# Attention over chosen chunks and a gated feed-forward: twenty-two loads issued by GpSimd in joined packets, and a new order table

## Chip, cores and metric

The kernel runs on one core of a Trainium2 chip. The metric is device time in microseconds of one execution; a profiled execution shows, beside its own time, the span from the first to the last instruction of the program. The engines are TensorE (PE; its weight loads are listed as PEld), VectorE (DVE), ScalarE (ACT), GpSimd (POOL) and SyncE (SP), which only issues transfers. Each engine works off its own queue in order. Transfers run on 16 DMA engines that all queues share.

## What is computed

Inputs are q, k, v of shape 4 x 8 x 768 x 64 (batch, heads, sequence, head size), and the weights of a feed-forward with 512 inputs and 1536 hidden values, all in float32.

```python
k_min, k_max = k_chunks.min(axis=3), k_chunks.max(axis=3)      # 24 chunks of 32 keys
ub = sum(maximum(q * k_min, q * k_max), axis=-1)               # bound of each query on each chunk
ub = where(causal, ub, -1e9); top_chunks = argsort(ub)[..., -6:]
scores = where(sel & (pos[:, None] >= pos[None, :]), scale * q @ k.T, -1e9)
x = softmax(scores) @ v                                        # as 3072 tokens x 512
out = (sigmoid(x @ w_gate) * (x @ w_val)) @ w_out
```

So each query attends, causally, to the six chunks with the highest bounds, and the result goes through the gated feed-forward.

## The kernel before

The 24 blocks of 128 queries (4 batches of 6) are put into eight units u0 to u7 of three blocks (u2 has two of its own and one more). The first block of each batch needs no choice of chunks; the functions `load_first` and `first` handle it. The first blocks of batches 0 to 2 are u0, that of batch 3 is joined to u2. For a unit the stages are:

- load queries and keys; turn them so that the head size lies on the partitions. u1 and u2 (batch 0) are loaded in wide rows (`load_wide`, tiles k0_u1 to q3_u2), copied (kn, qn) and turned on TensorE (kT, qT). Batches 1 to 3 are loaded in blocks of 32 x 32 (`load_blocks`, k00_1 to q11_3, runs of 128 B) and turned on VectorE.
- smallest and largest key of each chunk (kx, kcr), the bounds (ub), the six largest (mx), and from these a bias that is written beside the queries as extra rows (hqm) and meets a pattern beside the keys (hkp), so that the score product itself puts chunks out that were not chosen.
- scores (sc), exponent on ScalarE (exp), causal mask on GpSimd (cm), sums with the values (pv; the values are loaded by `load_v` as v_b_i and cast on GpSimd as v16), division (rz, x), turn (xps, xT).
- feed-forward: gate product g, value product v_u, tanh on ScalarE, product hg on VectorE, output product o0 to o2 in three pieces, eviction osb, store out. Weights come as wg0 to wg2, wv0 to wv2, wo0 to wo2, 512 KB each as landed, cast to float16 on their way by transfers that GpSimd issues. u4 with u5, and u6 with u7, share their gate and value products in a scheme with seven products in place of eight.

For a first block of batch b: kf0, kf1, qf0, qf1 (halves of the heads) and vf are its loads, kfT and qfT the turns, scm and scf mask and scores, expf, pvf, rzf, xf, xpsf, xTf the rest as above; xTf copies the result into u0's input.

Every step is entered with `plan.add(name, {engine: cost...}, emit, ...)`. Nothing is planned at run time: the text `ORDER` lists all 1893 entries by name, with the engine behind `@` where it is not the first one given in `add`, and behind `:` the slots of the buffers that the entry is the first to use. `plan.order()` emits them in that order, and each engine's queue is the sequence of its own entries. The costs in `add`, and the due times `prio`, were used to draw the table and do not act otherwise. Buffers matter for loads: there are two large landing buffers (`big`: u1, u2, and then the key and query blocks of a batch) and six for values and first blocks (`v`); a load whose buffer still has readers waits, and the loads behind it on that queue wait with it.

In the table before, SP issues 107 transfers: all key, query and value loads and all stores but the last. GpSimd issues only the nine weights. The first gate product, g_u0_0, has 54 TensorE entries ahead of it, among them twelve score groups of u1; wg0 and wv0 stand at places 21 and 23 of GpSimd's queue.

## Time and profile before

| | |
|---|---|
| median of 3 runs | 287.46 us (287.25 to 287.63) |
| profiled execution | 287.56 us, span 285.8 us |
| HBM read, written | 30.67 MB, 6.29 MB |
| SP's queue: packets, MB, share of 16 engines | 118448, 27.47, 45.3% |
| GpSimd's queue: packets, MB, share of 16 engines | 4752, 4.72, 10.2% |
| granted TensorE clock | 0.998 |

How to read the views: busy time is the union of an engine's instructions. Idle time is put down to what released the engine. The 40 slices of a row show the busy share of each slice in tenths, a slice being 7.1 us. A row of the view by stretch gives start and end, length, then busy time and count for PE, PEld, DVE, ACT and POOL, the granted clock, the DMA share and GB/s. A row of a tile or line gives the shortest, median and longest duration in ns and the first and last start in us, and "to landing" the time from an issue to the end of its transfer.

### The profile page before, as it was taken

To read this page: it belongs to the slowest core of one execution; us is meant where nothing else is said; L and a number is where in the kernel's file an instruction comes from. 1 tells how busy PE (TensorE), PEld (TensorE's weight loads), DVE (VectorE), ACT (ScalarE), POOL (GpSimd) and SP (SyncE) were. 2 spreads that over 40 slices of the span, in tenths; PEclk is the share of its full clock that TensorE was granted. 3 is DMA by queue.
4 is the path that set the end of the run, shared out by engine and by line. 5 is a ranking of instruction groups with operands and counts; after the bars stand their busy time and mean duration, and the time that the engine had idled before them with its cause. 6 is when DMAs were issued, how large, how long until landed. Compare 5 with 4: busy or idle time off the path is not lost.

```text
span 285.8 us, 7062 instructions
## 1 busy us (share of the span) xinstructions
PE 268.1 (94%) x2626; PEld 170.8 (60%) x2626; DVE 230.8 (81%) x626; ACT 213.2 (75%) x452; POOL 120.7 (42%) x199
## 2 busy tenths in 40 slices
PE   1677899999999899999999999999999999999995
PEld 0554566656666557777657776665667555555542
DVE  3588967659996998898978988898998778799842
ACT  4979887667858798989998978689899324766311
POOL 6479688214672688875674732350212000000000
PEclk9999999999999999999999999999999999999999
DMA  6999999999999999998031000100000020100005
GB/s 167 278 225 204 208 209 209 212 174 197 181 214 148 212 214 214 217 181 149 30 85 74 4 2 0 39 37 2 38 3 2 0 110 2 73 37 3 0 17 204
DMA packets 123377, 32.69 MB, mean 114 GB/s; under 512 B 111440, under 2 KB 120400, under 8 KB 123344
## 3 DMA queue, kind: packets, MB, share of 16 engines
q1 hardware_dynamic: 118448, 27.47, 45.3%
q0 software_dynamic: 4752, 4.72, 10.2%
q8 instruction: 20, 0.33, 0.5%
q14 instruction: 13, 0.11, 0.1%
q10 hardware_dynamic: 144, 0.07, 0.1%
HBM read 30.67 MB, written 6.29 MB: 129 GB/s over the span
## 4 chain that ended last, share of the span: by engine, by line
PE 74%; DMA 5%; SPq 4%; DVE 3%; ACT 3%; issue 1%; POOL 0%; DVEq 0%
PE o_u L962 19%; PE sc_u L848 10%; PE v_u L931 8%; PE g_u L931 8%; PE pv_u L881 6%; SPq L537 3%; PE sug_u6u L1041 3%; PE suv_u6u L1041 3%; PE sug_u4u L1041 3%; PE suv_u4u L1041 3%; DMA k<-in_k_dram 2%; DMA q<-in_q_dram 2%; PE ube_u L787 2%; PE xps_u L908 1%; PE srv_u6u L1041 1%; PE srg_u6u L1041 1%
## 5 line engine op out<-in xcount | busy, mean ns | idle before, releaser
L859 ACT ACTIVATE att_u<-sc_u 128x512 f16<-128x512 f32 (+3 forms) x184 | 91.4, 556 | 16.2 <-PE sc_u L848 15.0
L962 PE MATMUL o_u<-wo,hg_u 128*128 128x512 f16 x216 | 52.8, 379 | 0.0
L865 POOL TENSOR_SCALAR_AFFINE_SELECT att_u<-att_u 128x384 f16<-128x384 f16 (+1 forms) x56 | 29.1, 529 | 48.7 <-ACT att_u L859 45.8
L931 PE MATMUL v_u<-xT_u,wv 128*128 128x384 f16 x192 | 39.1, 326 | 0.0
L931 PE MATMUL g_u<-xT_u,wg 128*128 128x384 f16 x192 | 39.0, 326 | 0.0
L962 PEld LDWEIGHTS <-hg_u 128*128 128x128 f16 x216 | 20.4, 98 | 20.1 <-issue 0.6
L939 ACT ACTIVATE gate_u<-g_u 128x384 f16<-128x384 f32 x48 | 23.7, 498 | 8.7 <-PE g_u L931 8.5
L943 DVE SCALAR_TENSOR_TENSOR hg_u<-gate_u,v_u 128x384 f16<-128x384 f16 x48 | 25.3, 539 | 5.6 <-PE v_u L931 2.3
L848 PE MATMUL sc_u<-hqe,hke 128*128 128x128 f16 (+2 forms) x220 | 28.7, 243 | 1.2 <-DVE kx_u L561 0.9
L848 PE MATMUL sc_u<-hqo,hko 128*128 128x128 f16 (+2 forms) x220 | 27.6, 243 | 0.5 <-DVE hg_u L943 0.5
L881 PE MATMUL pv_u<-v,att_u 128*128 128x65 f16 x640 | 27.3, 193 | 0.7 <-POOL att_u L865 0.6
L881 PEld LDWEIGHTS <-att_u 128*128 128x128 f16 x640 | 24.7, 98 | 4.9 <-POOL att_u L865 1.1
L931 PEld LDWEIGHTS <-wv 128*128 128x128 f16 x192 | 17.8, 98 | 10.5 <-issue 0.5
L931 PEld LDWEIGHTS <-wg 128*128 128x128 f16 x192 | 18.0, 98 | 10.0
L848 PEld LDWEIGHTS <-hke 128*128 128x128 f16 x220 | 16.7, 98 | 6.8 <-issue 1.6
L848 PEld LDWEIGHTS <-hko 128*128 128x128 f16 x220 | 16.8, 98 | 6.3 <-ACT att_u L859 0.6
L971 ACT ACTIVATE osb_u<-o_u 128x512 f32<-128x512 f32 x17 | 10.1, 606 | 9.3 <-PE o_u L962 9.3
L962 PE MATMUL o_u<-wo,hgp_u 128*128 128x512 f16 (+1 forms) x72 | 17.0, 370 | 0.0
L553 POOL CAST v<-v 128x512 f16<-128x512 f32 x23 | 13.8, 611 | 4.1 <-DMA v<-in_v_dram 3.8
L900 DVE TENSOR_TENSOR x_u<-pv_u,rz_u 128x384 f16<-128x384 f32 (+1 forms) x28 | 14.6, 528 | 0.7 <-PE xps_u L908 0.3
L342 ACT COPY xT_u<-xps_u 128x384 f16<-128x384 f16 (+1 forms) x22 | 10.1, 474 | 5.2 <-PE xps_u L908 5.1
L346 POOL CAST k<-k 128x768 f16<-128x768 f32 x9 | 7.5, 833 | 13.9 <-DMA k<-in_k_dram 13.8
(215 smaller groups left out, 597.3 us busy)
## 6 DMA issues: line engine op xcount, KB each, us to landing
v<-in_v_dram SPq DMA_DIRECT2D x23, 256.0 KB, 4.5
out_dram<-osb_u SPq DMA_DIRECT2D x23, 256.0 KB, 2.1
k<-in_k_dram SPq DMA_DIRECT2D x12, 384.0 KB, 6.8
q<-in_q_dram SPq DMA_DIRECT2D x12, 384.0 KB, 5.4
wg<-in_moe_w_gate_dram POOLq DMA_DIRECT2D x3, 512.0 KB, 8.9
wv<-in_moe_w_val_dram POOLq DMA_DIRECT2D x3, 512.0 KB, 10.0
wo<-in_moe_w_out_dram POOLq DMA_DIRECT2D x3, 512.0 KB, 9.1
kf<-in_k_dram SPq DMA_DIRECT2D x8, 128.0 KB, 3.4
```

The source lines that it names most:

```text
L342: nc.scalar.copy(o, i)
L553: plan.add(f"v16_{b}_{ib}", {POOL: pool(H * D)}, lambda e: nc.gpsimd.tensor_copy(v16[b % 2][:, ib, :, 0:D], at(t)), reads=[t], writes=[("v ...
L848: nc.tensor.matmul(at(t)[:, o:o + 128 * m], hk[b % 2][e_][:, p, 128 * jb:128 * jb + 128], hq[u.side][e_][:, p, 128 * x:128 * (x + m)], sta ...
L859: plan.add(f"exp_{u.name}_{h}_{y}", {ACT: act(n)}, lambda e, t=t, att=att, b0=b0, n=n: nc.scalar.activation(at(att)[:, b0:b0 + n], at(t), ...
L865: nc.gpsimd.affine_select(out=dv, in_=dv, compare_op=ALU.is_ge, fill=0.0, base=0, pattern=[[0, u.m], [1, 128]], channel_multiplier=-1)
L881: nc.tensor.matmul(at(pv)[:, last, x, :], at(att)[:, c:c + 128], v16[b % 2][:, jb, h, :], start=(jb == 0), stop=(jb == ib))
L900: plan.add(f"x_{u.name}_{p}", {DVE: dve(u.t)}, lambda e: nc.vector.tensor_tensor(at(x_).rearrange("p a (e d) -> p e a d", e=2), at(pv)[:, ...
L931: nc.tensor.matmul(at(t), w16[:, c, 128 * fb:128 * fb + 128], at(u.xt)[:, c, :], start=(c == 0), stop=(c == 3))
L939: plan.add(f"tanh_{u.name}_{fb}", {ACT: act(T)}, lambda e, g=g, gate=gate: nc.scalar.activation(at(gate), at(g), AF.Tanh, scale=0.5), read ...
L943: plan.add(f"hg_{u.name}_{fb}", {DVE: dve(T)}, lambda e, w_=w_, gate=gate, hg=hg: nc.vector.scalar_tensor_tensor(at(hg), at(gate), 1.0, at ...
L962: nc.tensor.matmul(at(o), hgs[c][1][1]()[:, 128 * tb:128 * tb + 128], wo16[:, fc, lo:hi], start=(c == 0), stop=(c == NFB - 1))
L1041: nc.tensor.matmul(at(t), left[i](c), right[i](c), start=first and c == 0, stop=c == 1, skip_group_check=not first)
```

## The change

Three helpers that issue loads now take an engine: a load by GpSimd is issued with `single_packet=True`, so that the pieces which one DMA engine has to move are joined in one packet. Which loads go there is written in the table. The table itself is drawn anew: 185 of the 1893 entries change their engine (22 of them loads), and nearly all their places.

```diff
+    def read(e, o, i):
+        if e == SP:
+            nc.sync.dma_start(o, i)
+        else:
+            nc.gpsimd.dma_start(o, i, single_packet=True)
...
-                plan.add(f"{n}f_{b}", {SP: (550, 550)}, lambda e, t=t[n], src=src: nc.sync.dma_start(
+                plan.add(f"{n}f_{b}", {SP: (550, 550), POOL: (930, 930)}, lambda e, t=t[n], src=src: read(e, 
...
-                    plan.add(f"{n}f{e_}_{b}", {SP: (550, 550)}, lambda e, t=t[n], src=src, e_=e_: nc.sync.dma_start(
+                    plan.add(f"{n}f{e_}_{b}", {SP: (550, 550), POOL: (750, 750)}, lambda e, t=t[n], src=src, e_=e_: read(e, 
...
-                plan.add(f"{'kq'[j]}{p}_{u.name}", {SP: (450, 450)}, lambda e, j=j, p=p, src=src: nc.sync.dma_start(
+                plan.add(f"{'kq'[j]}{p}_{u.name}", {SP: (450, 450), POOL: (800, 800)}, lambda e, j=j, p=p, src=src: read(e, 
...
-        plan.add(f"v_{b}_{ib}", {SP: (450, 450)}, lambda e: nc.sync.dma_start(
+        plan.add(f"v_{b}_{ib}", {SP: (450, 450), POOL: (930, 930)}, lambda e: read(e, 
```

The start of the table, before and after (the first load of each, and the place of the first weights and of the first products of the feed-forward):

```diff
-tri0 ap1 ident epat0:0 ident16 tri k2_u1:0 kn_u1_2:0 kT_u1_2:0 kt_u1_2:0 q1_u2:1 vf1_1:1 epat kcr0 kx0_u1_2
...
-hq1_u1_2@POOL wv0 apt0_u1:0 rzf_1_1:1 xf_0_0:0 hk1_u1_0@ACT kn_u2_2:6 qf16_3:0 hq0_u1_1 expf_0_1:1 kT_u2_2:6 kx0_u2_2
...
-wv1 cm_u1_1 v16_0_1 kx0_u2_0 v16_0_3 exp_u1_2_1 g_u0_0:4,0,0 exp_u1_0_2 tanh_u0_0 kfT_3:7 v_u0_0:3 mx1_u1 kx0_u2_3
+hq0 epat0:0 k1_u1:0 ident kn_u1_1:0 kT_u1_1:0 v10 k0_u2:1 kf1_2:0 kf0_2 q1_u1 k0_u1@POOL kn_u1_0:1 q2_u1@POOL kf1_0:1
+epat kn_u2_0@POOL:2 hkp001 qf1_0:2 q1_u2 hkp101@ACT kT_u2_0:1 kt_u2_0@DVE:0 kx1_u2_0:0 qn_u1_1@POOL:3 qT_u1_1:2 hk0_u2_0
...
+hkf1@ACT kT_u1_3:0 kx1_u1_3 expf_0_0 qT_u2_1:3 qf1_3:5 qf1_1 wg0 hk0_u1_0@ACT pvf_0_0:4 expf_0_1:2 hq1 qfT_1:2 qT_u2_0:7
...
+vc_1 qn_u2_2:1 qfT_2:2 xpsf_0_0:7,0 qf16_2:5 wv0 kx0_u1_3 kt_u1_3@DVE:2 xTf_0_0 kcr_u1@POOL qm_u1_1@ACT qm_u1_0@ACT
...
+hqm0_u1_0 kf0_3@POOL:0 g_u0_0:3,0,0 v_u0_0:1 g_u0_1:4,1,1 kt_u2_1@DVE:2 kx1_u2_1 ubn1_u1 v_u0_1:2 hkf0@ACT hkp110@ACT
...
+qm_u2_1@ACT qm_u2_2@ACT k11_1:0 v_0_2:5 v_u0_3:6 tanh_u0_3 exp_u1_2_2 v_0_3:1 kf1_3 exp_u1_2_0 hkp010 hg_u0_2 hg_u0_3
```

In queue order, GpSimd's loads are k0_u1, q2_u1, k2_u2, qf0_0, q0_u2, qf0_1, q2_u2, qf0_2 (all ahead of wg0), q3_u2 (ahead of wv0), kf0_3, v_0_1, vf_3, v_0_4, v_1_2, v_1_0 and seven more values of batches 1 to 3. wv1 and wg1 follow wv0 with three entries of other work among them. SP keeps 85 transfers; behind its first 24 loads come k11_1, v_0_2, v_0_3 and kf1_3. g_u0_0 has 42 TensorE entries ahead of it, none of them scores of u1; v_u0_0 comes right behind it.

More of the change, by code (lines that the diff above doesn't have):

```diff
@@ new lines @@
+vc_1 qn_u2_2:1 qfT_2:2 xpsf_0_0:7,0 qf16_2:5 wv0 kx0_u1_3 kt_u1_3@DVE:2 xTf_0_0 kcr_u1@POOL qm_u1_1@ACT qm_u1_0@ACT
+scm_2:4,1 pvf_0_1:0 pvf_1_0:6 pvf_1_1:7 scf_2:2 qT_u2_2:2 kxf1:1 expf_2_0 k1_u2 rzf_0_1:1 xf_0_1:1 xpsf_0_1:5 pvf_2_0:0
+rzf_1_1:0 xf_1_1:2 xTf_0_1 wv1 rzf_1_0:1 hk0_u1_2@POOL qf16_3:4 rzf_2_0:0 xf_2_0:0 xpsf_1_1:4 kT_u2_3:7 expf_2_1:3
+qf_u2_2 hq0_u1_1@POOL pvf_2_1:3 xTf_1_1 wg1 xf_1_0:1 rzf_2_1:0 hkp100 kcr_f@POOL xpsf_2_0:5 kn_u2_1@DVE:3 xf_2_1:2
+xTf_2_0 ub_u1:1,0 qm_u2_0@POOL:0 xpsf_1_0:2 ubn0_u1:0 xpsf_2_1:4 xTf_2_1 hk0_u1_3@POOL hk1_u1_3@POOL hq1_u2_2 hkp011@ACT
@@ new lines @@
+exp_u1_1_0 sc_u1_0_0:5,0 exp_u1_0_0 qm_u2_3@ACT sc_u1_0_2:4 sc_u1_3_2:3 g_u0_4:2,1,4 sc_u1_3_1:7 v_u0_4:1 exp_u1_3_1
+exp_u1_0_2 sc_u1_1_2:0 sc_u1_0_1:5 g_u0_5:6,0,5 v_u0_5:7 exp_u1_3_2 exp_u1_1_2 tanh_u0_5 sc_u1_2_1:4 sc_u1_1_1:3 hg_u0_5
+wv2 ub_u2:0,6 tanh_u0_4 exp_u1_1_1 g_u0_6:2,2,6 v_u0_6:7 g_u0_7:3,3,7 ap1_u1 apt1_u1 hg_u0_4 exp_u1_0_1 ubn1_u2:0
+ubn0_u2 hq1_u1_1@DVE exp_u1_2_1 hqm1_u1_0@ACT cm_u1_0 tanh_u0_6 hqm1_u1_2@ACT cm_u1_1 k10_1 mx1_u2:0 hq0_u2_0@POOL
+cm_u1_3 v16_0_1 v16_0_3 v16_0_2 pv_u1_0:5 tanh_u0_7 pv_u1_1 sc_u1_4_1:4,0 sc_u1_7_2:1,3 sc_u1_4_0:0 exp_u1_7_2
@@ L270 @@
+P3v_u6u7_5 C1v_u6u7_5 o1_u6_0 o1_u6_2 P4v_u6u7_5 o1_u7_1 hg_u6u7_1_11 hg_u6u7_1_5 o2_u7_1 hg_u6u7_0_11 o0_u7_0:0,1
+o1_u7_0 o2_u7_0 hg_u6u7_0_5 o2_u6_2 o0_u7_2:5,2 osb_u7_0@DVE out_u7_0 osb_u6_2 out_u6_2 o2_u6_0 osb_u6_0@DVE osb_u7_1
+out_u7_1 out_u6_0 o2_u6_1 osb_u6_1 out_u6_1 o1_u7_2 o2_u7_2 osb_u7_2@DVE out_u7_2 o0b_u7_2:6 o1b_u7_2 o2b_u7_2 osbb_u7_2
+outb_u7_2@ACT
 """
```

328 lines of the change are left out of this document (156 added, 172 removed).

## The prediction

> **What bounds the kernel now.** I read the page first (busy times, the 40 slices), then busy time by stretch, then the timeline at the places where TensorE waits, and last the landings of single loads.
>
> ```profile
> span 285.8 us, 7062 instructions
> PE 268.1 (94%) x2626; PEld 170.8 (60%) x2626; DVE 230.8 (81%) x626; ACT 213.2 (75%) x452; POOL 120.7 (42%) x199
> PE   1677899999999899999999999999999999999995
> DMA  6999999999999999998031000100000020100005
> ```
>
> ```profile
> 0.00:33.00 33.00, 20.06 (x191) 13.80 (x192) 22.30 (x69) 26.64 (x51) 23.96 (x48) 1.00 0.97 218
> 33.00:50.00 17.00, 16.96 (x210) 11.29 (x209) 12.68 (x56) 14.44 (x34) 12.38 (x23) 1.00 1.29 207
> 50.00:130.00 80.00, 78.80 (x843) 51.60 (x841) 67.98 (x202) 63.82 (x136) 47.66 (x76) 1.00 1.08 197
> 130.00:180.00 50.00, 50.00 (x625) 33.93 (x624) 43.88 (x123) 44.06 (x89) 26.36 (x40) 1.00 0.18 44
> 180.00:280.00 100.00, 99.94 (x745) 58.75 (x744) 82.11 (x179) 63.96 (x143) 10.37 (x16) 1.00 0.07 27
> 280.00:285.80 5.80, 2.36 (x21) 1.44 (x19) 1.90 (x3) 0.28 (x1) 0.00 (x0) 0.92 0.60 226
> ```
>
> The columns of the second view are the stretch, its length, then busy us of TensorE matmuls, weight loads, VectorE, ScalarE and GpSimd, the granted clock, the DMA share and GB/s. TensorE is the bound: of 17.7 us in which it does nothing (285.8 - 268.1), 12.94 lie in the first 33 us, 1.20 between 50 and 130 us and 3.44 behind 280 us. The arithmetic is the same in the changed kernel, so its time is this TensorE work plus whatever idle time the new order leaves. The end (last output products, eviction, store) keeps its form in the new table; its 3.44 us I leave as they are. What can move is the head, and the 1.20 us.
>
> The head is bound by loads and by the engines that turn them, in this way:
>
> ```profile
> 0.00:5.00 5.00, 0.88 (x3) 0.50 (x3) 1.54 (x5) 1.86 (x3) 3.62 (x11) 1.00 0.48 128
> 5.00:10.00 5.00, 1.37 (x7) 1.38 (x8) 1.74 (x4) 4.44 (x6) 1.33 (x2) 1.00 1.03 285
> 10.00:15.00 5.00, 3.99 (x24) 2.95 (x22) 3.75 (x9) 4.58 (x8) 3.31 (x5) 1.00 1.08 256
> ```
>
> ```profile
> 5.45 0.56 DVE L561 TENSOR_REDUCE kcr<-kT_u 128x12 f32<-128x384 f32 x1 [2.90 <-ACT kt_u L342]
> ...
> 32.51 0.27 DVE L344 COPY xT_u<-xpsf 128x256 f16<-128x256 f16 x1
> ```
>
> ```profile
> 33.00 0.81 PE L931 MATMUL g_u<-xT_u,wg 128*128 128x384 f16 x4
> 33.65 0.60 PE L589 MATMUL kfT<-ident,kf 128*128 128x128 f32 x4
> 34.26 0.82 PE L931 MATMUL v_u<-xT_u,wv 128*128 128x384 f16 x4
> 34.92 0.81 PE L931 MATMUL g_u<-xT_u,wg 128*128 128x384 f16 x4
> ```
>
> From 5 us on the DMA engines are full; only the first 5 us have room (share 0.48), because one queue, SP's, issues everything. The first gate product g_u0_0 starts at 33.00 us, just behind the last piece of its input that VectorE copies (32.51 + 0.27); the first value product v_u0_0 at 34.26 us, just behind its weights:
>
> ```profile
> L492 POOL DMA_DIRECT2D wg<-in_moe_w_gate_dram x1: 995/995/995, 21.8 to 21.8; - x1
> ...
> DMA to landing us min/median/max: 9.1/9.1/9.1
> ```
>
> ```profile
> L493 POOL DMA_DIRECT2D wv<-in_moe_w_val_dram x1: 751/751/751, 23.3 to 23.3; - x1
> ...
> DMA to landing us min/median/max: 10.9/10.9/10.9
> ```
>
> ```profile
> L492 POOL DMA_DIRECT2D wg<-in_moe_w_gate_dram x1: 740/740/740, 31.4 to 31.4; - x1
> ...
> DMA to landing us min/median/max: 7.3/7.3/7.3
> ```
>
> ```profile
> L493 POOL DMA_DIRECT2D wv<-in_moe_w_val_dram x1: 747/747/747, 32.1 to 32.1; - x1
> ...
> DMA to landing us min/median/max: 10.0/10.0/10.0
> ```
>
> wg0 lands at 21.8 + 9.1 = 30.9, wv0 at 23.3 + 10.9 = 34.2; wg1 at 38.7, wv1 at 42.1. So a weight of 512 KB lands 7.3 to 9.1 us after its issue with nothing ahead of it on Pool's queue, and 3.3 to 3.4 us after the one ahead of it otherwise. From 33 us on TensorE is full (16.96 of 17.00).
>
> **The change, part by part. (a) Loads to Pool.** SP loses 22 of its 107 entries, Pool gains 22. Price on SP, and the nearest on Pool:
>
> ```profile
> L527 SPq DMA_DIRECT2D kq_u<-in_k_dram x8: 435/469/505, 0.8 to 20.9; - x8
> L547 SPq DMA_DIRECT2D v<-in_v_dram x23: 375/803/4636, 22.0 to 142.4; - x23
> L492 POOL DMA_DIRECT2D wg<-in_moe_w_gate_dram x3: 740/788/995, 21.8 to 41.1; - x3
> ```
>
> No load of this kind was ever issued by Pool here, nor one in joined packets. I take 0.8 us each, by the weights' median, with 0.74 and 0.995 as ends: 17.6 us of Pool's time (16.3 to 21.9). In the table Pool hands over 25 other entries (ScalarE +7, VectorE +18), at some 0.5 us each about 12 us, so Pool goes from 120.7 to about 126 us, VectorE from 231 to about 238 of 286: each has room on average, and this part costs nothing while TensorE has other work ready. What waits behind a Pool issue are Pool's casts and causal masks; in the head, eight loads stand before wg0.
>
> On how the two queues share the engines: the Trainium skill, "DMA: Bandwidth & Descriptors", section "Issuing engines are not separate DMA queues", says that transfers issued by any engine run on the same 16 DMA engines and that a second issuer only saves sequencer time. By that rule the move buys no bandwidth beyond the half empty first 5 us, and the case of no change below is the one it speaks for; the share of 1.03 to 1.08 in the rows from 5 to 15 us agrees.
>
> **(b) The head in the new order.** Pool's queue up to wg0: 14 entries that are not loads, by their rows about 9.5 us (the two pattern fills 2.0, one mask copy 1.46, one clamp 1.0, the rest 0.3 to 0.6), eight loads at 0.8 make 6.4, the start at 0.8 us, and about 1 us of waiting for a query load and for a turned query: wg0 is issued at 17.6 instead of 21.8. Then a cast, two small fills, one query copy and one load, some 2.2 us, and wv0 goes at about 20.7. wg0 lands at 24.9 to 26.7, wv0 3.3 later, at 28.2 to 30.0. The other condition is the last copied piece of the input: VectorE has 58 entries to do up to there, against 60 before. Without a single wait behind the first turned tile this is 5.45 + (22.30 - 1.54), or 26.2 us; with every wait of before 32.8. I take the middle, 29.5, because loads land earlier but the chain load, turn, copy, score, exp, sum, divide, turn, copy is as long as it was. g_u0_0 then starts at 29.5 and v_u0_0 at 30.15 with its weights there.
>
> That is not all gain: the new order does less TensorE work before v_u0_0. Twelve score groups of u1 and one turn of keys, which stood ahead, now come behind.
>
> ```profile
> 0.00:33.00 33.00, 3.29 (x24) 1.85 (x24) 1.00 0.97 218
> ```
>
> This is busy time of the scores' line alone in the head: 3.29 us for these 24 matmuls. Streaming alone they need less, 12 groups of 384 columns on average at 0.16 us (a product of four such matmuls takes 0.65, 34.92 less 34.26), or 1.95. With 0.60 for the turn of keys the start that would change nothing is 34.26 - 0.60 - (1.95 to 3.29), or 30.4 to 31.7, middle 31.0. So the head gives **0.85 us** (ends: v_u0_0 at 33.45, if VectorE waits as it did, is a loss of 3.0 against 30.4; at 28.2 it is a gain of 3.5 against 31.7).
>
> **(c) Weights in a row.** wv1 and wg1 are issued at about 21.8 and 23.6, not 32.1 and 31.4, so four weights run in a row. At 3.3 apart they land at about 32.4 and 35.7. g_u0_4 needs wg1; it stands behind v_u0_0, six more products (4.55 with it) and seven score groups (1.9 by 3.29 / 12 each): 30.15 + 6.45 = 36.6. It is just in time: cost 0, or 2.5 us at a spacing of 5 (rival C).
>
> **(d) Keys and values of the later units.** k11_1, the first block load of keys (128 B runs), may start as soon as u1's landing buffer is free and the 24 loads ahead of it on SP are issued (at 0.47 to 0.80 us each 11 to 19 us), say at 18 us; v_0_2, v_0_3 and kf1_3 queue behind it on SP; before, these values went ahead of it.
>
> ```profile
> L537 SPq DMA_DIRECT2D k<-in_k_dram x1: 1431/1431/1431, 33.4 to 33.4; - x1
> ...
> DMA to landing us min/median/max: 14.6/14.6/14.6
> ```
>
> ```profile
> L537 SPq DMA_DIRECT2D k<-in_k_dram x4: 1431/6047/12317, 33.4 to 55.2; - x4
> ...
> DMA to landing us min/median/max: 7.5/16.4/24.2
> ```
>
> By 14.6 us beside weights it lands at 32.6, the two values by 35 (256 KB at 212 GB/s is 1.2 us each), and pv_u1_0, which needs them cast, is due near 43: cost 0; at 24.2 it is not (rival D).
>
> **(e) The middle.** Eleven of the values no longer stand in SP's queue among key and query blocks, so a block that TensorE waited for in 80 to 100 us can come sooner. Of the 1.20 us I count 0.35 as gained (ends: all 1.20, or a loss of as much again, since the whole table is drawn anew).
>
> **Sum.** -0.85 - 0.35 = -1.2 us. The profiled execution took 287.56 us (span 285.8 and 1.76 around it), 0.10 above the median of 287.46. So 287.56 - 1.2 - 0.10 gives **286.3 us**.
>
> **Rivals. A, larger gain:** VectorE runs with few waits (28.0) and v_u0_0 starts at 28.6: 2.4 in the head, 1.2 in the middle, 283.9. For it: loads come from two queues in the first 5 us. Against it: DMA is full from 5 us on.
>
> **B, no change:** the head is bound by bytes, whoever issues them; earlier weights only take from the loads that feed VectorE, which waits as long as before, less what the first 5 us give. 287.4.
>
> **C, slower, weights pile up:** wg1, fourth in a row beside loads and key blocks, holds g_u0_4, with all of TensorE behind it. It decides from a spacing of 3.75 us (36.6 less 29.1 for wv0, halved for two weights); at 5 us wg1 lands at 39.1, 2.5 late: 287.5 - 1.2 + 2.5 = 288.8. For it: the pair wg1, wv1 took 10.7 us before. Against it: 3.3 and 3.4 between neighbours.
>
> **D, slower, values behind k11_1:** at 24.2 us it lands at 42.2, the values at 44.6, two casts of 0.61 in Pool's order end at 45.8, some 2.8 late for pv_u1_0 at 43, and Pool's masks with them: 289.1. It decides from a landing behind some 39 us.
>
> ```profile
> L553 POOL CAST v<-v 128x512 f16<-128x512 f32 x23 | 13.8, 611 | 4.1 <-DMA v<-in_v_dram 3.8
> ```
>
> **E, slower, Pool pays more or the middle loses:** an issue costs over 0.995 because Pool is held up, or the redrawn middle adds idle time: 1 to 3 us; with 2 of it, and the head's 0.85 kept, 288.6. The Trainium skill, "SBUF — State Buffer", section "SBUF: two separate sides", warns that descriptors made by GpSimd starve while VectorE runs a two-port copy; it quotes 620 ns becoming 3100, which as an estimate from that page would put some 2.5 us on an unlucky issue. The spread here, 740 to 995 ns beside a busy VectorE, is a tenth of that.
>
> **Chances.** The forecast as told (285.4 to 286.8) 0.26, A 0.18, B 0.13, C 0.15, D 0.15, E 0.13. A measurement of this kernel can tell some 0.2%, 0.57 us, from no change. So faster 0.44, same 0.13, slower 0.43. Range 283.7 to 290.5: it takes in all but the far ends of A, C, D and E.
>
> **What would show it.** v_u0_0 at 30.2 or before with more than 20 us of TensorE work done by 33 us bears out (b); wv0 landing by 30 and wg1 by 36 bear out (c); no wait of TensorE at the first sums of u1 near 43 bears out (d); Pool's loads at 0.74 to 1.0 us bear out (a). The forecast is wrong if TensorE idles over 0.5 us between 33 and 50 us, if Pool's issues take over 1.2 us, or if the idle time of 50 to 180 us grows over 2 us.

## The result, and the profile after

| | before | after |
|---|---|---|
| median, 20 executions each | 286.82 us (285.26 to 288.20) | 288.59 us (286.49 to 290.06) |
| profiled execution, span | 287.56 us, 285.8 us | 288.12 us, 286.4 us |

The ratio of after to before is 1.006 [1.0041, 1.0079]: the change makes the kernel slower, by 1.2 to 2.3 us. The 20 executions of before put its median at 286.82 us, 0.64 below the 287.46 of the three from which the prediction added up. The two profiles differ by less, 0.56 us: the profiled execution of before lies 0.7 us above its median, that of after 0.5 us below. A second profile of before, taken with the experiments, has a span of 284.4 us, and both are used below.

Busy times of after, and the row of TensorE over 40 slices:

```profile
span 286.4 us, 7079 instructions
PE 268.5 (94%) x2626; PEld 170.9 (60%) x2626; DVE 236.7 (83%) x644; ACT 218.3 (76%) x459; POOL 122.9 (43%) x196
PE   2778899989998999999999999999999999999995
DMA  7999999999999879279140200103000020002005
```

The head of the row is fuller than before (2778 against 1677), and a few slices behind it are not. The view by stretch of after, with the columns of before, says how much:

```profile
0.00:33.00 33.00, 22.05 (x192) 14.45 (x193) 24.74 (x77) 26.42 (x49) 26.60 (x48) 1.00 1.07 233
33.00:50.00 17.00, 16.37 (x195) 11.16 (x193) 12.46 (x53) 15.46 (x38) 12.38 (x23) 1.00 1.27 225
50.00:130.00 80.00, 76.80 (x857) 50.56 (x852) 70.50 (x197) 66.96 (x143) 50.16 (x76) 1.00 0.95 176
130.00:180.00 50.00, 50.00 (x621) 33.91 (x620) 46.09 (x141) 40.31 (x80) 23.18 (x34) 1.00 0.24 55
280.00:286.40 6.40, 3.23 (x26) 1.93 (x24) 1.25 (x2) 0.94 (x3) 0.00 (x0) 1.00 0.59 222
```

TensorE is idle 10.95 us of the first 33 against 12.94 before, 0.63 against 0.04 from 33 to 50, and 3.20 against 1.20 from 50 to 130 us. The head gives and the middle takes. The middle again, 40 to 130 us, first of before and then of after:

```profile
40.00:130.00 90.00, 88.78 (x982) 58.20 (x980) 74.73 (x231) 71.81 (x155) 55.67 (x91) 1.00 1.11 198
```

```profile
40.00:130.00 90.00, 86.80 (x997) 57.85 (x997) 79.53 (x232) 76.47 (x165) 56.63 (x88) 1.00 0.99 181
```

In these 90 us VectorE has 4.8 us more to do and ScalarE 4.7 (79.53 - 74.73, 76.47 - 71.81). TensorE waits for them, and for late loads that reach it through them. The waits of TensorE, from the timeline of after (start, busy us, instruction, and in brackets the idle time ahead of it and who ended it):

```profile
29.93 0.50 PE L937 MATMUL v_u<-xT_u,wv 128*128 128x384 f16 x2 [0.90 <-DMA wv<-in_moe_w_val_dram]
36.50 0.50 PE L937 MATMUL g_u<-xT_u,wg 128*128 128x384 f16 x2 [0.63 <-ACT att_u L865]
63.35 0.37 PE L887 MATMUL pv_u<-v,att_u 128*128 128x65 f16 x7 [0.83 <-POOL v L559]
81.31 0.28 PE L854 MATMUL sc_u<-hqe,hke 128*128 128x256 f16 x1 [0.36 <-DVE hqe L344]
92.19 0.32 PE L854 MATMUL sc_u<-hqo,hko 128*128 128x384 f16 x1 [0.89 <-POOL hqo L346]
95.04 0.34 PE L914 MATMUL xps_u<-ident,x_u 128*128 128x128 f16 x3 [0.46 <-DVE x_u L906]
123.48 0.32 PE L937 MATMUL v_u<-xT_u,wv 128*128 128x384 f16 x1 [0.66 <-DVE hg_u L949]
```

The last five, 63 to 123 us, make 3.20 us. Before had only two waits of TensorE behind 33 us (line waited for, total us, times, longest us):

```profile
PE pv_u L881 <- POOL att_u L865: 0.6, 1, 0.6
PE sc_u L848 <- DVE hg_u L943: 0.5, 1, 0.5
```

Three of the five can be followed back. The wait at 63 us goes back to the value v_0_5, for which GpSimd's casts waited. Its row and landing (the longest of the loads of values in this window) are

```profile
L507 SPq DMA_DIRECT2D v<-in_v_dram x1: 1702/1702/1702, 55.3 to 55.3; - x1
DMA to landing us min/median/max: 4.8/5.8/6.8
```

SP issued it at 55.3, behind three blocks of keys, and it landed at 62.1. The wait at 92 us begins at VectorE:

```profile
87.97 0.98 DVE L567 TRANSPOSE_TENSOR_REDUCE kcr<-k 128x24 f32<-128x768 f32 x1 [1.92 <-DMA k<-in_k_dram]
```

VectorE stood still for 1.92 us until the last key block of batch 2 had landed (issued at 79.86, landed at 87.85), with the last bound products of u3 behind it in its order; GpSimd waited for these, TensorE for GpSimd. The wait at 123 us comes behind a clamp that takes 2.34 us:

```profile
119.07 2.34 DVE L583 TENSOR_SCALAR qm_u<-qf_u 128x768 f32<-128x768 f32 x1
```

### The profile page after: what moved, and what is told of

Its sections match the earlier page's. It is cut to its first block, busy times and chain, and to the rows that moved or that the text cites. A ratio compares the mean times of both kernels' runs of the same rounds, so it can differ in the third digit from the quotient of the medians.

```text
span 286.4 us, 7079 instructions
## 1 busy us (share of the span) xinstructions
PE 268.5 (94%) x2626; PEld 170.9 (60%) x2626; DVE 236.7 (83%) x644; ACT 218.3 (76%) x459; POOL 122.9 (43%) x196
## 3 DMA queue, kind: packets, MB, share of 16 engines
q1 hardware_dynamic: 102224, 22.88, 38.6%
## 4 chain that ended last, share of the span: by engine, by line
PE 70%; DMA 10%; DVE 6%; ACT 5%; SPq 4%; POOL 3%; issue 2%; DVEq 0%; POOLq 0%; ACTq 0%
PE o_u L968 19%; PE sc_u L854 9%; PE v_u L937 7%; PE g_u L937 6%; PE pv_u L887 5%; DMA wv<-in_moe_w_val_dram 3%; DMA k<-in_k_dram 3%; PE sug_u4u L1047 3%; PE suv_u4u L1047 3%; PE suv_u6u L1047 3%; PE sug_u6u L1047 3%; DMA v<-in_v_dram 2%; PE ube_u L793 2%; SPq L543 2%; SPq L507 2%
## 5 line engine op out<-in xcount | busy, mean ns | idle before, releaser
L865 ACT ACTIVATE att_u<-sc_u 128x512 f16<-128x512 f32 (+3 forms) x184 | 89.4, 551 | 13.8 <-PE sc_u L854 13.2
L968 PE MATMUL o_u<-wo,hg_u 128*128 128x512 f16 x216 | 53.6, 379 | 0.0
L871 POOL TENSOR_SCALAR_AFFINE_SELECT att_u<-att_u 128x384 f16<-128x384 f16 (+1 forms) x56 | 31.2, 568 | 50.7 <-ACT att_u L865 46.4
L854 PE MATMUL sc_u<-hqo,hko 128*128 128x128 f16 (+2 forms) x220 | 27.6, 243 | 0.9 <-POOL hqo L346 0.9
L854 PE MATMUL sc_u<-hqe,hke 128*128 128x128 f16 (+2 forms) x220 | 27.2, 243 | 0.4 <-DVE hqe L344 0.4
L977 ACT ACTIVATE osb_u<-o_u 128x512 f32<-128x512 f32 x18 | 10.7, 602 | 14.9 <-PE o_u L968 14.9
L816 DVE MAX8 mx_u<-ubn_u 128x8 f32<-128x8 f32 (+16 forms) x152 | 12.8, 158 | 0.2
L567 DVE TRANSPOSE_TENSOR_REDUCE kcr<-k 128x24 f32<-128x768 f32 x12 | 11.3, 950 | 1.9 <-DMA k<-in_k_dram 1.9
```

The source lines that it names most:

```text
L816: nc.vector.max(at(mx)[:, e_, j, :], at(ubn)[:, e_, j, 0:max(8, u.seen[j])])
L854: nc.tensor.matmul(at(t)[:, o:o + 128 * m], hk[b % 2][e_][:, p, 128 * jb:128 * jb + 128], hq[u.side][e_][:, p, 128 * x:128 * (x + m)], sta ...
L865: plan.add(f"exp_{u.name}_{h}_{y}", {ACT: act(n)}, lambda e, t=t, att=att, b0=b0, n=n: nc.scalar.activation(at(att)[:, b0:b0 + n], at(t), ...
L871: nc.gpsimd.affine_select(out=dv, in_=dv, compare_op=ALU.is_ge, fill=0.0, base=0, pattern=[[0, u.m], [1, 128]], channel_multiplier=-1)
L968: nc.tensor.matmul(at(o), hgs[c][1][1]()[:, 128 * tb:128 * tb + 128], wo16[:, fc, lo:hi], start=(c == 0), stop=(c == NFB - 1))
```

## Experiments

The columns of idle time are those of TensorE from the view by stretch. The ratio is the recorded estimate against the runs of before on the same chip, whose medians ran from 285.83 to 287.14 us, so it is not the quotient of two medians of this table. A profile is one execution, and lies up to 1.3 us to either side of its kernel's median (e1_values_sp 294.01 against 295.27, e5_new_to_70_v 288.15 against 287.02): a difference in idle time of less than that between two kernels is weak evidence. Idle time is not all that a kernel loses either: for the same 2626 matmuls TensorE is busy for 268.5 us in after and 273.1 in e1_all_sp.

| kernel | median us | ratio to before | idle 0 to 40 | idle 40 to 130 |
|---|---|---|---|---|
| before | 286.82 | | 12.95 | 1.22 |
| before, second profile | 286.24 (one) | | 12.57 | 0.51 |
| after | 288.59 | 1.006 [1.0041, 1.0079] | 11.58 | 3.20 |
| e1_all_sp | 298.13 | 1.0369 [1.0329, 1.0409] | 12.51 | 7.21 |
| e1_values_sp | 295.27 | 1.0272 [1.0231, 1.0312] | 11.19 | 7.04 |
| e1_head_sp | 292.99 | 1.0209 [1.0175, 1.0243] | 11.07 | 4.70 |
| e1_not_joined | 289.51 | 1.008 [1.0045, 1.0115] | 11.56 | 3.47 |
| e2_new_head | 288.67 | 1.0053 [1.0015, 1.0092] | 11.85 | 2.65 |
| e2_new_middle | 295.24 | 1.03 [1.0246, 1.0354] | 11.37 | 7.01 |
| e2_old_table_pool | 314.73 | 1.0963 [1.0904, 1.1022] | 20.69 | 6.84 |
| e2_one_value | 288.10 | 1.0046 [1.0009, 1.0083] | 12.28 | 2.64 |
| e3_keys_late | 288.28 | 1.006 [1.0031, 1.009] | 11.12 | 3.28 |
| e3_three | 287.14 | 1.002 [0.9988, 1.0052] | 11.46 | 3.46 |
| e3_new_head_b | 289.48 | 1.01 [1.0067, 1.0134] | 11.90 | 3.04 |
| e4_values_first | 288.43 | 1.0051 [1.0016, 1.0085] | 11.54 | 4.12 |
| e4_five | 288.11 | 1.0028 [0.9996, 1.0061] | 11.30 | 2.47 |
| e5_new_to_70 | 287.16 | 1.0054 [1.0031, 1.0078] | 10.36 | 2.44 |
| e5_new_to_70_v | 287.02 | 1.0042 [1.0017, 1.0067] | 11.74 | 3.29 |
| e6_pool_back | 291.35 | 1.018 [1.0146, 1.0214] | 10.71 | 3.48 |
| e6_old_engines | 294.25 | 1.0259 [1.0218, 1.0299] | 10.62 | 6.88 |

### Who issues the loads

Three kernels keep the new table and give loads back to SP at their places: all 22, the eleven values v_0_1 to v_3_5, or the eleven others (ten loads of the head, and vf_3).

```diff
-k0_u1@POOL
-qf0_1@POOL:4
...
-v_0_1@POOL:4
-v_3_5@POOL:3
+k0_u1
+qf0_1:4
...
+v_0_1:4
+v_3_5:3
```

A fourth keeps them on GpSimd and leaves out the joining.

```diff
-            nc.gpsimd.dma_start(o, i, single_packet=True)
+            nc.gpsimd.dma_start(o, i)
```

> The changed kernel's table, but all 22 loads issued by SP at their places in the table, as before the change. Theory T (the new table costs the time, in waits of TensorE between 60 and 130 us; the loads on GpSimd are no loss): not faster than the changed kernel, ratio to the kernel before 1.006 to 1.025, because SP issues 107 transfers one after the other again and the first value product starts later than 29.9 us. Rival P (the loads on GpSimd cost the time, through its issues of 0.7 to 0.95 us or through the joined packets): ratio falls to 0.998 to 1.002.

> The changed kernel with only the eleven values v_b_i back on SP; eleven head loads stay on GpSimd. T: ratio to the kernel before 1.006 to 1.015, head as in the changed kernel (first value product near 29.9 us), the values land later behind key and query blocks, idle time of TensorE between 60 and 130 us of 3.2 us or more. P, if the values' issues between the causal masks cost it: ratio 0.998 to 1.003 and idle time there under 2 us.

> The changed kernel with only the eleven loads of u1, u2 and the first blocks back on SP; the eleven values stay on GpSimd. T: the gain of 1.4 us in the first 33 us goes, ratio 1.009 to 1.018. P, if the head's issues cost it: ratio 0.998 to 1.004.

> The changed kernel with the 22 loads on GpSimd in ordinary, not joined packets. T: joining matters little, ratio 1.003 to 1.010. Rival J (joined packets hold each DMA engine and so keep SP's loads waiting): ratio 0.997 to 1.002, SP's values land sooner beside GpSimd's. Rival K (joined packets save DMA time): slower, 1.010 or more, with more DMA time on GpSimd's queue than 15.4%.

With all of them on SP the ratio to before is 1.0369 in place of 1.006, some 9 us more (0.031 x 287); with the values there it is some 6 more, with the others some 4. So loads by GpSimd are no loss in this table: without them it would be 3.7% slower than before. All three ratios lie beyond what T allowed (1.025, 1.015 and 1.018): the loads are worth more than it said. In the run with the head's loads on SP the first value product starts at 32.5 us in place of 29.9, and TensorE waits 1.76 us at 59.5 and 1.20 at 67.4. The trace of the run with the values on SP shows one place, in two loads of values on SP's queue and in TensorE's timeline:

```profile
L511 SPq DMA_DIRECT2D v<-in_v_dram x2: 1872/7254/12637, 21.0 to 33.8; - x2
DMA to landing us min/median/max: 10.7/13.7/16.8
```

```profile
45.70 0.47 PE L891 MATMUL pv_u<-v,att_u 128*128 128x65 f16 x10 [3.06 <-POOL v L563]
```

Behind k11_1 the issue of one value takes 12.64 us; the next goes out at 33.8 and lands 10.7 us later, at 44.5, and TensorE waits 3.06 us for its cast. That is rival D of the prediction, near the place that it named (43 us). In the changed kernel the same two issues take 6.38 and 5.17 us, and the second value lands at 37.8. There v_0_1, which stands ahead of k11_1 on SP in this run, is issued by GpSimd (at 34.2 us), and k11_1 goes out at 18.0 in place of 19.6. That this one value makes the difference was not tried.

What the joining does can't be told from nothing (1.008 [1.0045, 1.0115] against 1.006 [1.0041, 1.0079]). Nor do the profiles differ in packets. The rows of GpSimd's queue, of after and then without the joining, give packets, MB and share:

```profile
q0 software_dynamic: 6224, 9.31, 15.4%
```

```profile
q0 software_dynamic: 6224, 9.31, 15.3%
```

Before, this queue had 4752 packets. So the 22 loads are 1472 packets on GpSimd's queue, with or without the joining, where on SP's they are 16224 (118448 - 102224). Neither J nor K was tested by this edit as far as the profile counts packets.

```profile
L509 POOL DMA_DIRECT2D v<-in_v_dram x11: 897/907/952, 34.2 to 155.1; - x11
L509 POOL DMA_DIRECT2D kq_u<-in_q_dram x4: 702/716/737, 2.4 to 19.2; - x4
```

These are rows of after: 0.70 to 0.95 us for every load that GpSimd issues, none held up.

> The old table, word for word, with the same 22 loads issued by Pool in joined packets at the places at which SP issued them. It is the change without its table. Theory M says nothing sharp of it: eleven loads of the head add some 9 us of Pool's time ahead of the first weights, whose issue would go from 21.8 to 24 us or later, so 1 to 3 us slower than before by the head, and up to 1 us given back by the values. Rival P2 (loads by Pool are a gain by themselves, since SP's queue gets shorter): 0.5 to 1.5 us faster than before.

Here the edit is the reverse, the old table with the same 22 marked `@POOL`. It takes 314.73 us, 28 more than before, much beyond what either theory said. GpSimd issues the first weight at 26.0 us in place of 21.8, and the head alone has 20.69 us of idle time. A place in SP's order is no place in GpSimd's, which has casts and masks ahead of it: who issues a load can't be judged apart from where it stands.

### Which part of the table

Two kernels join one table's first 55 us to the other's order behind it. The cut is at o0_u0_1; every entry that the first part has already is left out of the second, and 14 and 13 buffers get another number so that the parts fit.

The first has the new table's part in front, the second the old one's.

```diff
 sc_u2_0_1:4 exp_u2_2_1 rzf_3_1:0 hg_u0_11 o2_u0_0
-o0_u0_1:1,1 osb_u0_0 k01_1 k00_1 k16_1_3@ACT:2
+hq0_u2_1@POOL hk1_u2_2@POOL k01_1 k00_1 xTf_3_0@ACT
...
```

> The new table up to the second output product of u0 (the first 55 us), then the old table's order for all that is left, with its values on SP; twelve buffers are renumbered and eight entries shifted a few places so that the two parts fit. Theory M (the new head is worth 1.4 us of TensorE's idle time, the new middle costs 2 to 3): this is faster than before by about 1.4 us, 0.995 of it, with TensorE's idle time of the first 40 us near 11.6 us and no wait over 1 us from 60 to 130 us other than at the seam. Rival R (the head gives nothing in the median, since its earlier weights and loads make something later slower whatever the order): within 0.5 us of before or slower.

> The old table up to the second output product of u0, then the new table's order, with its eleven values mostly on Pool's queue; thirteen buffers renumbered, four entries shifted. Theory M: slower than before by 2 to 3 us (1.007 to 1.010), slower than the changed kernel by about 1.4 us, with the waits at 92, 95 and 123 us still there. Rival R: as before, within 0.5 us, since the middle's order is not what costs.

R's number came (1.0053), but neither kernel could answer. By stretch, the first shows:

```profile
60.00:80.00 20.00, 17.35 (x145) 11.35 (x144) 13.28 (x23) 11.43 (x26) 6.92 (x14) 0.91 1.00 195
80.00:100.00 20.00, 20.00 (x220) 12.70 (x219) 19.60 (x61) 15.78 (x31) 13.12 (x20) 1.00 0.92 152
100.00:130.00 30.00, 30.00 (x385) 20.70 (x384) 27.18 (x94) 27.08 (x59) 22.97 (x35) 1.00 0.99 195
```

Behind the seam there is no idle time at all from 80 to 130 us, where after has 2.37. But the seam itself costs 2.65 us between 60 and 80, TensorE waiting for exponentials of entries that were left over from the old order, and the granted clock falls to 0.91. A kernel that has lost 2.65 us at 70 us also has 2.65 us more for whatever would have been late at 90. In the second, TensorE waits 4.71 us for values at 69 us.

> The new table up to apt1_u2 (about 50 us) and the old table's order behind it, a seam that needs no entry shifted and renumbers eight buffers. The first seam had waits of its own of 3 us at 63 to 70 us, so it said nothing of the head. Theory H1 (the new head is worth the 1.4 us that the two profiles show): 285.4 to 286.0 beside a before of 286.8, unless this seam waits too. Theory H2 (the profile of before shows a head some 1 us worse than usual; the gain in most executions is 0.3 to 0.6 us): 286.3 to 286.8.

A seam at apt1_u2, with no entry shifted and eight buffers renumbered, waits 1.86 us at 54.8 and 1.18 at 56.6: slower still (1.01), and nothing behind it. The last pair spreads the seam: between about 60 and 82 us each entry's place goes over from the new table's to the old one's, weighted by how far along it is.

> The new table up to about 62 us, the old table's order word for word from mx1_u3 (about 82 us) on, and between them each entry at a place that goes over from its new place to its old one, so that no engine has a heap of left-over entries at one seam as in the two hybrids before. Fifteen of the 22 loads are Pool's; the seven later values are SP's again. Theory M3 (the head of the new table is a gain of about 0.7 us, and its waits from 80 to 130 us, 2.4 of the 3.2 us, belong to its order there): TensorE's idle time from 80 to 130 us is below 1.2 us, as in the old table, and the time is 286.0 to 286.9, at or below before. Rival S (the waits come with the earlier head, whatever order follows): idle time of 80 to 130 us over 2 us and a ratio to before of 1.004 or more.

> The same with v_0_5 on Pool's queue behind wo1 and k16_1_0 behind the values' casts. M3: the same or up to 0.5 us faster, if the wait near 63 us does not come back as a wait for ScalarE's exponentials as it did in the two runs before; S: 1.004 or more.

M3's first number (below 1.2 us) came true in the first run and was missed by 0.12 us in the second; its time came in neither. Idle time from 80 to 130 us is 1.16 and 1.32 us, as in before (1.19, 0.33) and not as in after (2.37); but 40 to 80 us has 1.28 and 1.97 us where the profiles of before have 0.03 and 0.18, and the ratios stay at 1.0054 and 1.0042, which is the time that S said, without its idle time of over 2 us. So a better order from 82 us on does not give the time back.

### The second profile of before

> The kernel before, profiled once more. H2 expects less than 12.95 us of TensorE's idle time in the first 40 us, 11.5 to 12.5; H1 expects 12.7 to 13.2 again.

12.57 us of idle time in the first 40 us, just above H2's range and below H1's. With e2_new_middle, which has the old head too (11.37), the old head has 12.30 us on average over three profiles; the new head, over the 14 profiles that have it with its loads on GpSimd, 11.37 (10.36 to 12.28). In idle time the head's gain is some 0.9 us, not the 1.37 of the one pair of profiles. Even that is rough. The three lowest of the 14 (10.36, 10.62 and 10.71 us) come with more busy time of TensorE (270.1, 272.1 and 270.0 us against 268.5 in after), and e1_head_sp has 11.07 us of idle time although its first value product starts 2.6 us later than in after.

### The waits one by one

The first edit puts v_0_5 on GpSimd's queue (in all kernels of this part but e3_keys_late):

```diff
-v_0_5:1
+v_0_5@POOL:1
...
```

> The changed kernel with one more value, v_0_5, on Pool's queue, right behind wo1, so that it no longer stands in SP's queue behind three key blocks. Theory M (the wait of 0.99 us at 63 us is that value's late landing): that wait is gone and the time is 0.6 to 1.0 us below the changed kernel's, 288.0 or so. Rival (something next in line is late by as much, or the weights on Pool's queue come later): within 0.3 us of the changed kernel, with a wait of the same size within 10 us behind.

The wait at 63 us is gone from the profile (60 to 80 us: 20.00 of 20.00 us busy), and the ratio goes from 1.006 to 1.0046: 0.4 us where M said 0.6 to 1.0, and within both intervals. The second edit moves VectorE's work on the late block (in e3_keys_late, e3_three and e4_five):

```diff
-k10_2 kx0_2_3 k16_2_2@DVE:5 kx0_2_2 exp_u3_3_1
+k10_2 exp_u3_3_1
...
-apt1_u3 cm_u3_1
+apt1_u3 kx0_2_3 k16_2_2@DVE:5 kx0_2_2 cm_u3_1
```

> The changed kernel with three of VectorE's entries, the two chunk reductions and one cast of unit 2's last key block (kx0_2_3, k16_2_2, kx0_2_2), moved behind apt1_u3. In the changed kernel VectorE stood idle for 1.92 us up to 87.97, until that block had landed at 87.85, with the last two bound products of u3 behind it. Theory M1 (the waits of TensorE at 92.19, 1.05 us, and at 95.04, 0.62 us, are this wait handed on): both shrink to below 0.3 us and the kernel is 1.0 to 1.7 us faster than the changed one, 287.2 or so beside a before of 286.8. Rival L (TensorE is held there by VectorE's amount of work, 83% busy, not by the place of one wait): the waits stay or move by less than 10 us, and the time falls by less than 0.4 us.

VectorE's wait of 1.92 us and TensorE's of 0.89 at 92 us are gone as M1 said; the one at 95 us, which should have fallen below 0.3, is not. The time did not move (1.006), and a wait 10 us earlier has grown:

```profile
82.39 0.28 PE L854 MATMUL sc_u<-hqe,hke 128*128 128x256 f16 x1 [0.95 <-DVE hqe L344]
95.12 0.29 PE L914 MATMUL xps_u<-ident,x_u 128*128 128x128 f16 x2 [0.51 <-DVE x_u L906]
```

The first of these was 0.36 us in after. This is L's number for the time; M1 was right of the wait at 92 us alone. The third edit, in e3_three and e4_five, exchanges u5's clamps:

```diff
-qm_u5_0@ACT:0
+qm_u5_0:0
...
-qm_u5_2
+qm_u5_2@ACT
```

> As the run with the keys late, with v_0_5 on Pool behind wo1 as well, and the two clamps of u5 given back to the engines they had in the old table (qm_u5_2 to ScalarE, qm_u5_0 to VectorE), since the clamp of 2.34 us on VectorE at 119 us stands ahead of the product for which TensorE waits 0.82 us at 123.48. Theory M1: the waits at 63, 92, 95 and 123 us are gone, 1.0 + 1.7 + 0.8 at most, 2 to 3 us off the changed kernel: 285.6 to 286.6, level with before or just below it. Rival L: at most 1.2 us off, and others of VectorE's waits in their place.

The waits at 92 and 123 us are gone and the ratio is 1.002 [0.9988, 1.0052], the lowest of all, still not under 1. In its profile another wait is as long as the three that should go (0.83, 0.89 and 0.66) together. This profiled execution lies 1.0 us above the kernel's median, so the wait need not be so long in most. Now v_0_5 is on GpSimd, and its cast stands behind GpSimd's cast of a key block, which landed at 62.06 there:

```profile
62.21 0.82 POOL L346 CAST k<-k 128x768 f16<-128x768 f32 x1 [4.69 <-DMA k<-in_k_dram]
```

```profile
64.56 0.31 PE L887 MATMUL pv_u<-v,att_u 128*128 128x65 f16 x5 [2.33 <-POOL v L559]
```

The fourth edit moves that cast (in both kernels that follow), and e4_five has all edits and three places of VectorE's order:

```diff
-k16_1_0:5
...
-v16_0_5 v16_0_4
+v16_0_5 v16_0_4 k16_1_0:5
...
-hg_u1_3 ap0_u3 apt0_u3:0 hqm0_u3_0@DVE
+ap0_u3 apt0_u3:0 hqm0_u3_0@DVE hg_u1_3
...
-kx1_2_1:0
...
-hg_u1_9 x_u3_0:1
+x_u3_0:1 hg_u1_9 kx1_2_1:0
```

> The changed kernel with v_0_5 on Pool's queue behind wo1, and k16_1_0, Pool's cast of unit 1's last key block, moved behind the casts of v_0_5 and v_0_4. In the run with three edits that cast waited for its block until 62.06 us, and the two casts of values behind it made TensorE wait 2.49 us at 64.56. Theory M2 (values behind key blocks, first in SP's queue and then in Pool's, are what TensorE waits for near 63 us): no wait over 0.4 us from 55 to 75 us, and 0.8 to 1.3 us off the changed kernel, ratio to before 1.002 to 1.003. Rival (the wait belongs to the loads' bandwidth at that time, whatever the order): a wait of 0.5 us or more is still there, and the ratio stays at 1.005 or above.

> All edits so far together (v_0_5 on Pool, k16_1_0 behind the values' casts, the last key block's reductions behind apt1_u3, u5's two clamps exchanged between ScalarE and VectorE), and three places in VectorE's order: hg_u1_3 behind hqm0_u3_0, hg_u1_9 and kx1_2_1 behind x_u3_0, for the waits at 81 and 95 us. Theory M (the new table's loss is a handful of places in two engines' queues where something waits behind a key block or a long entry): TensorE's idle time of 60 to 130 us falls from 3.20 to under 1 us, and the time to 286.0 to 286.6, level with before or 0.2% under it. Rival L (VectorE's amount of work; a wait removed comes back elsewhere): idle time of 60 to 130 us stays over 2 us, and the ratio to before is 1.003 or more.

With the values' casts ahead of that block's there is no wait for values near 63 us in either run. In its place stands ScalarE, in the profile of e4_five so:

```profile
64.03 0.33 PE L854 MATMUL sc_u<-hqo,hko 128*128 128x256 f16 x2 [1.09 <-ACT att_u L865]
```

```profile
60.00:80.00 20.00, 18.61 (x196) 11.73 (x195) 18.35 (x42) 16.50 (x35) 12.11 (x19) 1.00 1.08 208
80.00:100.00 20.00, 19.23 (x193) 12.49 (x192) 18.79 (x49) 15.09 (x33) 12.52 (x19) 1.00 1.02 193
```

VectorE is busy for 18.35 and 18.79 of 20 us. Edits against five waits leave 2.47 us of idle time of 3.20; the ratio is 1.0028 [0.9996, 1.0061]. M's under 1 us fell; L's over 2 us held, and its ratio of 1.003 or more was just missed. This profile lies 1.1 us below the kernel's median, so most executions lose more. In e4_values_first, where M2 allowed no wait over 0.4 us near 63 us, the same wait for ScalarE is 1.09 us, with another of 0.66 ahead of it.

### Who does the work that GpSimd gave away

Between about 43 and 135 us, 17 entries that the old table had on GpSimd go back there (e6_pool_back), or all 43 that have another engine than in the old table (e6_old_engines; the expectations say 48). Order and loads stay.

```diff
-hq0_u2_2
+hq0_u2_2@POOL
...
-k16_2_2@DVE:5
+k16_2_2:5
...
-hqm0_u5_0@DVE
+hqm0_u5_0
```

> The changed kernel's order and loads; in the stretch from about 43 to 135 us the 17 entries that Pool had in the old table and gave to ScalarE (11) or VectorE (6) go back to Pool, at their places. Theory W (the loads cost by what Pool gives away for them: VectorE and ScalarE have some 4 us more to do by 130 us each, and TensorE waits for them): idle time of 60 to 130 us below 1.5 us and a ratio to before of 1.002 or less. Rival N (Pool with both, its loads and its old work, is late instead; the wait is in each engine's order, not in who does what): TensorE waits as long or longer, now for Pool, ratio 1.005 or more.

> The same stretch, with all 48 of its entries (loads not counted) that changed their engine back on the old one: Pool gets 17 back, and ScalarE and VectorE exchange what they had exchanged. W: idle time of 60 to 130 us below 1.5 us, ratio 1.002 or less. N: 1.005 or more.

W fell as a remedy. With 17 entries back on GpSimd, VectorE and ScalarE have less to do and the waits between 60 and 100 us go from 2.54 to 0.54 us, but from 100 to 130 us they rise from 0.66 to 2.23, the largest of them for GpSimd:

```profile
60.00:80.00 20.00, 20.00 (x207) 12.61 (x205) 17.22 (x41) 15.47 (x32) 14.65 (x25) 1.00 1.09 218
80.00:100.00 20.00, 19.46 (x194) 12.66 (x192) 18.34 (x50) 14.48 (x33) 14.39 (x22) 1.00 1.05 186
100.00:130.00 30.00, 27.77 (x359) 18.99 (x357) 25.97 (x88) 22.55 (x49) 23.35 (x33) 1.00 0.69 134
```

```profile
112.66 0.50 PE L853 MATMUL sc_u<-hqe,hke 128*128 128x128 f16 x4 [1.46 <-POOL hke L345]
```

The median is 291.35 us; the idle time of 40 to 130 us, 3.48, explains little of it. Its profile has 2.0 us more idle time than after behind 280 us (5.20 against 3.17), where one store's issue took 2.21 us, and TensorE is busy for 1.5 us more (270.0 against 268.5). With all of them exchanged back the idle time is 6.88 us. Each entry's place was chosen for its engine's load, and GpSimd with its loads and its old work is late instead.

## Why the prediction was wrong

**(a), the price of a load on GpSimd, was right.** Forecast 0.8 us each, 0.74 to 0.995: the rows show medians of 0.72 to 0.93. The 22 come to 18.6 us (forecast 17.6; 11 x 0.907 + 4 x 0.716 + 3 x 0.778 + 2 x 0.816 + 0.840 + 0.927), GpSimd to 122.9 us (126), VectorE to 236.7 (238). What was not right is "this part costs nothing": room on average is not room between 40 and 130 us, where VectorE goes from 83% to 88% busy and ScalarE from 80% to 85% (74.73, 79.53, 71.81 and 76.47 of 90).

The prediction also took the DMA engines to be full from 5 us on. From 5 to 10 and from 10 to 15 us, after moves 310 and 329 GB/s where before moved 285 and 256:

```profile
5.00:10.00 5.00, 2.69 (x10) 1.90 (x11) 3.58 (x10) 4.35 (x6) 3.81 (x7) 1.00 1.16 310
10.00:15.00 5.00, 3.85 (x24) 3.08 (x23) 5.00 (x12) 4.21 (x10) 4.98 (x9) 1.00 1.08 329
```

Over these 10 us the 14 profiles of the new head with its loads on GpSimd have 282 to 320 GB/s. The six others have 259 to 271, the new head with its loads on SP and the old table with the loads on GpSimd among them. So a share of 1.03 to 1.08 did not mean that no more bytes could be moved, and the order and the issuer together gave more; which property of the loads does it was not tried.

The Trainium skill, "DMA: Bandwidth & Descriptors", section "Issuing engines are not separate DMA queues", says that a second issuer saves only the time of issuing. The extra bytes can be such saved time, but the step from the page to "no bandwidth" behind 5 us was wrong here; giving the 22 loads back to SP cost some 9 us in this table. The starved descriptors of the Trainium skill, "SBUF — State Buffer", section "SBUF: two separate sides", were not seen in the issues, the longest of which took 0.95 us; whether they lengthen a landing was not followed.

**(b), the head, was right in direction and size.** These rows of after answer it:

```profile
L492 POOL DMA_DIRECT2D wg<-in_moe_w_gate_dram x1: 756/756/756, 17.7 to 17.7; - x1
DMA to landing us min/median/max: 9.1/9.1/9.1
```

```profile
L493 POOL DMA_DIRECT2D wv<-in_moe_w_val_dram x1: 782/782/782, 20.7 to 20.7; - x1
DMA to landing us min/median/max: 9.2/9.2/9.2
```

wg0 at 17.7 (forecast 17.6), landed 26.8; wv0 at 20.7 (20.7), landed 29.9 (28.2 to 30.0); v_u0_0 at 29.93 (30.15), and 22.05 us of TensorE's work done by 33 (over 20). That the start came so near is in part luck: the last copied piece of the input was there at 27.6 us, not at 29.5, and the first gate product began at 28.2, so that wv0's landing alone, with 0.90 us of waiting, set the start that the sum had put down to VectorE. The gain, 0.85 in the sum, measures 1.37 us on the one pair of profiles and 0.9 on the average of all, in idle time.

**(c) was right to 0.6 us.** wv1 landed at 33.0 and wg1 at 36.5 (32.4 and 35.7); g_u0_4 began at 36.50 after 0.63 us of waiting, forecast 36.6 and 0. The timeline puts this wait down to an exponential of ScalarE, which ended at 36.50 too, so the trace can't tell the two apart. Rival C, 2.5 us, did not come.

**(d) was right in its cost.** k11_1, issued at 18.0 as forecast, took 17.0 us to land, at 35.0 (32.6), the values landed at 37.0 and 37.8 (35), and still nothing waits near 43 us: TensorE is busy in all of 40 to 60 us. Rival D's mechanism is real, as the run with the values on SP shows, and the price that it named, 2.8 us, was 3.06 there.

**(e), the middle, is the step that failed.** It counted 0.35 us as gained, between 1.20 gained and 1.20 lost. It measured 1.98 us lost by the pair of profiles (3.20 against 1.22 of idle time from 40 to 130 us) and 2.69 by the second profile of before, so that even the lower end was too near. The reason given, that values no longer stand among key blocks, was true of eleven values and not of the rest: v_0_5 stayed behind three blocks on SP. The reason on the other side, that the whole table is drawn anew, was named as the lower end and as rival E, and the sum counted nothing for it. What the step left out, in our reading, is that the old table's 1.2 us (0.5 in the second profile) was already the result of a close arrangement, from which a redrawn one can hardly gain. For it speaks that the old order behind either seam has no idle time at all from 80 to 130 us.

Of the prediction's own signs of being wrong, the first came (0.63 us of idle time from 33 to 50 us, where it allowed 0.5). The third stood at its bound of 2 us on the pair of profiles and beyond it by the second.

The terms then add up. Pair of profiles: head -1.37, middle +1.98, tail and rest -0.3, TensorE's busy time +0.32, together +0.6 (286.4 - 285.8). Against the second profile: -0.99 + 2.69 - 0.23 + 0.53 = 2.0 (286.4 - 284.4). The medians differ by 1.77. Of the rivals it is E, in its second half: 2 us of idle time in the redrawn middle, at 288.6 us, was the number that came (288.59). That it fits to 0.01 us is luck: E added 1.15 us to a median of 287.46, and the change added 1.77 to one of 286.82. E's first half, an issue held up, did not come.

**What is not settled.** Shown is where the time goes, that in this table it is neither the price of the loads nor, as far as the profiles show a difference, the joining, and that no single wait holds it: in the eleven kernels of the table above that have the new head and no more than single edits, a seam or the 17 entries against after, 40 to 130 us kept 2.4 to 4.1 us of idle time, whichever waits were taken away. Open is why so constant a rest stays. Two readings fit: TensorE, early by 0.9 us from the head, meets work that VectorE, ScalarE and the loads can't have ready sooner; or the places still to be found are many and small. Against the first speaks e1_head_sp, whose head is 2.6 us later than that of after: it still has 1.74 us of idle time from 80 to 130 us, behind two waits that make 2.96, where after has 2.37. Neither reading was tried by a run that leaves out the other. A table that keeps this head and is drawn with the landings of the key blocks as measured was not tried. No kernel here is shown to be faster than before.

## What to carry to other kernels

Judge a load on a second queue with the order in hand, by what it takes out of the first queue's way and what stands behind it on the second: the same 22 loads were worth 9 us in one table and cost 28 in another, neither of which was drawn for the other issuer. When an order written out for five engines is drawn anew, price the stretch that was nearly full before as a likely loss with its own term, from the engines' shares in that stretch rather than over the span. And take more than one profile where a gain of one microsecond is at stake: TensorE's idle time in the first 40 us was 12.95, 12.57 and 11.37 us in three executions of the old head, the last that of e2_new_middle.
